# The loads of batch 1 go through the Pool queue, in one order with the weights

## The chip, the cores and the metric

The kernel runs on one core of a Trainium2 chip. The metric is the device time of one execution in microseconds (us). A profile is one execution taken by the hardware profiler; its times count from the start of its span. Engines are named as the profile names them: PE is the matrix engine (PEld its weight loads), DVE the vector engine, ACT the scalar engine, POOL the GpSimd engine, SP the engine that here only issues DMAs. SPq and POOLq are the sequencers of SP and POOL, which wait and issue. DMA queue q1 is fed by SP, queue q0 by POOL, and the same 16 DMA engines serve both.

## The reference: sliding-window attention, then a gated feed-forward

```python
scores = scale * q @ k^T            # B=8, H=8, S=576, D=64
mask   = (0 <= i - j < 64)          # a causal window of 64
attn   = softmax(where(mask, scores, -1e9))
x      = (attn @ v) as [B*S, H*D]   # 4608 tokens x 512
h      = x @ w_in                   # 512 x 2048
out    = (h * clip(h + 3, 0, 6) / 6) @ w_out   # 2048 x 512
```

All inputs and the output are float32. The kernel computes in bf16 with float32 accumulation.

## The kernel before

**Tiles of tokens.** The 4608 tokens are cut into nine tiles of 512 (T = 0 to 8). Each tile has two stages on PE. `s1(T)` multiplies the transposed tokens xT by w_in in 16 column blocks (fc = 0 to 15, four matmuls each, line 530) and gates each block on ACT (line 537) and DVE (line 538) into gT. `s2(T)` multiplies gT by w_out (line 567) into four groups of 128 tokens (ts = 0 to 3). Both are Python generators: each step emits a few instructions, and the code that calls `run(m, n)` places the attention of a coming batch between the steps. The schedule is manual, so each engine does its instructions in the order in which the program lists them.

**Attention of a batch.** A batch has 576 positions, 512 main rows and 64 rest rows. The pieces are: casts of Q, K and V to bf16 on POOL (lines 286, 293, 247); transposes of Q and K on PE, `TT(bt, g)` for a pair of heads g and `RR(bt)` for the rest rows (lines 316, 298), copied out of PSUM by DVE and ACT; scores and exponentials, `S1_(g, half, bank)` (lines 353, 361), masked on DVE (line 371); weighted sums and division by their sum, `N_(bt, g)` (lines 383 to 405); and the transpose into xT, `X_(bt, g)` (line 416). Batches 0 and 1 are transposed on PE. From batch 2 on, Q and K are transposed by DMA, issued by SP: lines 276 to 282 for batch 2, pair by pair, and lines 269 to 274 for batch 3 and later, one transfer for Q and one for K.

**Tile 0.** Tile 0 needs only the main rows of batch 0, so the rest rows of batch 0 are deferred and done inside tile 0 by `RR(bt0)`, `rest_s`, `rest_n`, `rest_x`. During `s1(0)` PE does the first two `TT` of batch 1, and during `s2(0)` the rest of batch 1's attention. `s2(0)` runs in the order BY_PART: four steps with the first quarter of w_out (one for each ts), then four with the second quarter, and so on: 16 steps of four matmuls.

**Loads in tile 0.** The weights come through POOL's queue as four parts of w_in (512 columns each, lines 225 to 229) and four of w_out (512 rows each, lines 231 to 235); they are cast from float32 to bf16 on the way. Each part has 512 rows. Everything else comes through SP's queue, all float32: Q and K of batch 1 in halves of four heads (line 107, 512 rows of 1 KB each), the rest rows of batch 1 (line 113, `rst`, 512 rows of 256 B for Q and as many for K), the rest rows of batch 0 (line 151, three transfers of that kind), then V of batch 1 (lines 94 and 82, 512 rows of 256 B for each of nine transfers), then batches 2, 3, ... (line 94, 1024 rows of 256 B each).

**What sets the order.** The first halves of Q and K of batch 1 wait on SP until the second part of w_in has landed (lines 704, 705). POOL casts that half of Q, issues the first part of w_out, casts the half of K and issues the other three parts of w_out (lines 720 to 723). SP holds `rst` of batch 1, the second halves of Q and K and the rest rows of batch 0 until the first part of w_out has landed (lines 724, 725), and V until the third has (lines 726, 727). POOL casts `rst` (line 728), the second halves (729) and batch 0's rest rows (730). After V, SP issues the loads of batch 2, its transposes, the loads of batch 3, and so on. Staging tiles have one buffer each.

In `s2(0)` before, `RR(bt)` stands after four steps, the last two `TT` after eight.

Of the kernel before, what the change touches and what calls it, by code (L numbers as in the profile page):

```python
# [24 lines left out]
def kernel(  # L25
# [42 lines left out]
    def after(ins, dep, why):  # L68

        tc.add_manual_dep(  # L70
            ins.ins, dep.ins.name,
            mybir.DependencyInfo(mybir.DependencyClass.Sync, mybir.DependencyReason.DATA),
            reason=why,
        )
# [22 lines left out]
            ))  # L97
        return out

    def load_qk_for_pe(b, heads):  # L100
        qst = stage.tile([P, H, R * D], F32, name="qst", tag="qst")
        kst = stage.tile([P, H, R * D], F32, name="kst", tag="kst")
        rst = stage.tile([P, H, D], F32, name="rst", tag="rst")
        ins = []
        for h0 in range(0, H, heads):
            for dst, src in ((qst, q), (kst, k)):
                ins.append(nc.sync.dma_start(
                    out=dst[:, h0 : h0 + heads, :],
                    in_=src[b, h0 : h0 + heads, 0:SM, :].rearrange("h (p j) d -> p h (j d)", j=R),
                ))  # L110
            if h0 == 0:
                for i, src in enumerate((q, k)):
                    ins.append(nc.sync.dma_start(
                        out=rst[i * SR : (i + 1) * SR, :, :],
                        in_=src[b, :, SM:S, :].rearrange("h s d -> s h d"),
                    ))
        return (qst, kst, rst), ins

    def load_v_by_head(b):
        vst = stage.tile([P, KB, H, D], F32, name="vst", tag="vst")  # L120
        ins = load_blocks(vst, v, b, (KB - 1,), SR) + load_v(b, vst, 0, H)
        return vst, ins
# [23 lines left out]
    def load_rest_of_first():  # L146
        rst = stage.tile([P, H, D], F32, name="rst0", tag="rst0")
        rvst = stage.tile([P, H, D], F32, name="rvst", tag="rvst")
        ins = []
        for dst, p0, src in ((rst, 0, q), (rst, SR, k), (rvst, SR, v)):  # L150
            ins.append(nc.sync.dma_start(
                out=dst[p0 : p0 + SR, :, :], in_=src[0, :, SM:S, :].rearrange("h s d -> s h d"),
            ))
        return rst, rvst, ins

    stage0, ins0 = load_first()
    vst0 = stage.tile([P, KB, H, D], F32, name="vst", tag="vst")
# [67 lines left out]
    def load_w_in(f0, f1, g0, g1):  # L225
        return nc.gpsimd.dma_start(
            out=win16[:, g0:g1, f0:f1],
            in_=moe_w_in[g0 * P : g1 * P, f0:f1].rearrange("(g p) f -> p g f", p=P),
        )

    def load_w_out(c0, c1):
        return nc.gpsimd.dma_start(
            out=wout16[:, c0:c1, :],
            in_=moe_w_out[c0 * P : c1 * P, :].rearrange("(c p) j -> p c j", p=P),
        )
# [4 lines left out]
    class Batch:  # L240
        def __init__(self, b):
            self.b = b
            self.QT, self.KT = QT_ring[b % NQT], KT_ring[b % NQT]
            self.V = V_ring[b % NV]
# [181 lines left out]
    def rest_s(bt, u):  # L426
        st = ps_st.tile([P, 2, 512], F32, name=f"st{u}")
        for g in range(NG):
            for h in range(2):
                nc.tensor.matmul(  # L430
                    st[:, h, g * SR : (g + 1) * SR],
                    lhsT=bt.KT[h * D : (h + 1) * D, g, S - P : S],
                    rhs=bt.QT[h * D : (h + 1) * D, g, SM:S], start=True, stop=True,
                )
        nc.scalar.activation(out=pTr[:], in_=st[:, :, 0 : NG * SR], func=EXP, scale=scale)
        pv_ = pTr[:].rearrange("p h (g s) -> p (h g) s", s=SR)
        nc.vector.tensor_tensor(
            out=pv_, in0=pv_,
            in1=mask1[:, WINDOW : 2 * WINDOW].unsqueeze(1).to_broadcast([P, H, SR]), op=MULT,
        )  # L440

    def rest_n(bt, u):
        st = ps_st.tile([P, 2, 512], F32, name=f"st{u}")
        for h in range(2):
            o = st[:, h, :]
            for g in range(NG):
                nc.tensor.matmul(
                    o[0:SR, g * VW : (g + 1) * VW], lhsT=pTr[:, h, g * SR : (g + 1) * SR],
                    rhs=bt.V[:, KB - 1, 2 * g + h, :], start=True, stop=True,
                )  # L450
        for h in range(2):
            ov = st[0:SR, h, 0 : NG * VW].rearrange("p (g w) -> p g w", w=VW)
            rec = small.tile([P, KB], F32, name="rec")
            nc.vector.reciprocal(out=rec[0:SR, 0:NG].unsqueeze(2), in_=ov[:, :, D:VW])
            nc.vector.tensor_tensor(
                out=opr[0:SR, :, h, :], in0=ov[:, :, 0:D],
                in1=rec[0:SR, 0:NG].unsqueeze(2).to_broadcast([SR, NG, D]), op=MULT,
            )

    def rest_x(bt):  # L460
        tr = ps_st.tile([P, 2, 1024], BF16, name="st0")[:, 0, :]
        for g in range(NG):
            nc.tensor.transpose(
                out=tr[:, g * SR : (g + 1) * SR],
                in_=opr[0:SR, g, :, :].rearrange("p h d -> p (h d)"), identity=ident[0:SR, 0:SR],
            )
        acopy(
            out=xT[:, :, bt.b * S + SM : (bt.b + 1) * S],
            in_=tr[:, 0 : NG * SR].rearrange("d (g s) -> d g s", s=SR),
        )  # L470
# [89 lines left out]
    def s2(T, order):  # L560

        gT, accs = gTs[T], {}
        for ts, f0, f1 in order:
            if f0 == 0:
                accs[ts] = h_bank()[:] if T == 0 and ts > 1 else next(oa)
            for fc in range(f0, f1):
                nc.tensor.matmul(  # L567
                    accs[ts], lhsT=gT[:, fc, ts * P : (ts + 1) * P], rhs=wout16[:, fc, :],
                    start=(fc == 0), stop=(fc == NFC - 1),
                )  # L570
            if f1 == NFC:
                osb = osbp.tile([P, DM], F32, name="osb")
                acopy(out=osb[:], in_=accs[ts])  # L573
                u0 = T * TB + ts * P
                if T:
                    nc.sync.dma_start(out=out[u0 : u0 + P, :], in_=osb[:])
                else:
                    held.append((u0, osb))
            yield
# [4 lines left out]
    def run(gen, n=10 ** 6):  # L584
        for _ in range(n):
            if next(gen, "end") == "end":
                break
# [29 lines left out]
    def X_(bt, g, st=None):  # L617
        xt_pe(bt, g, h_tr() if st is None else ps_st.tile([P, 2, 1024], BF16, name=f"st{st}")[:, 0, :])()

    def TT(bt, g, banks=None):  # L620
        T_(bt, g, banks)
        do(bt, "q", g)
        do(bt, "k", g)
# [23 lines left out]
    bt.cast_v(vst0, 4, 6, pcopy)  # L647
    w_in.append(load_w_in(512, 1024, 0, NG))
    bt.cast_v(vst0, 6, 8, pcopy)
    w_in += [load_w_in(512 * i, 512 * (i + 1), 0, NG) for i in (2, 3)]  # L650
    pcopy(out=bt.V[0:SR, KB - 1, :, 0:D], in_=bt.V[SR:P, KB - 2, :, 0:D])

    def S0_(g, u):
# [46 lines left out]
    run(m, 1)  # L700


    st1, ins = load_qk_for_pe(1, 4)
    for x in ins[:2]:
        after(x, w_in[1], "the weights go first")
    bt0 = bt
    rst0, rvst0, insr = load_rest_of_first()
    vst1, insv = load_v_by_head(1)
    insv = insr[2:] + insv

    fill_v(1)
    nc.vector.tensor_copy(
# [5 lines left out]
        )  # L718
    bt, st = Batch(1), st1
    bt.cast_qk(st, 0, 0, 4, pcopy)  # L720
    w_out = [load_w_out(0, 4)]
    bt.cast_qk(st, 1, 0, 4, pcopy)
    w_out += [load_w_out(4 * i, 4 * i + 4) for i in (1, 2, 3)]
    for x in ins[2:] + insr[:2]:
        after(x, w_out[0], "the weights go first")
    for x in insv:
        after(x, w_out[2], "the weights go first")
    bt.cast_rest(st, pcopy)
    cast_pairs(bt, st, 4, 4)
    bt0.cast_rest((None, None, rst0), pcopy)  # L730
    run(m, 12)
    TT(bt, 0, oa_tr)
    run(m, 2)
    TT(bt, 1, oa_tr)
# [8 lines left out]
    def st_tr(u):  # L743
        t = ps_st.tile([P, 2, 1024], BF16, name=f"st{u}")
        return iter((t[:, 0, :], t[:, 1, :]))
# [5 lines left out]
    def S1_(g, u, bank):  # L751
        scores(bt, g, u, bank=bank)()
        if u:
            masked(bt, g)

    m = s2(0, BY_PART)
    S1_(0, 0, 0)
    S1_(1, 0, 1)
    run(m, 4)
    RR(bt, st_tr(0))  # L760
    run(m, 1)
    S1_(0, 1, 1)
    run(m, 1)
    S1_(1, 1, 0)
    run(m, 2)
    TT(bt, 2, st_tr(1))
    TT(bt, 3, st_tr(0))
    run(m, 1)
    S1_(2, 0, 1)
    run(m, 1)  # L770
    S1_(2, 1, 0)
    run(m, 1)
    S1_(3, 0, 1)
    run(m, 1)
    S1_(3, 1, 0)
    run(m, 1)
    RR(bt0, st_tr(1))
    run(m, 1)
    rest_s(bt0, 1)
    N_(bt, 0, st_pair(0))  # L780
    run(m, 1)
    rest_n(bt0, 1)
    N_(bt, 1, oa)
    run(m, 1)
    N_(bt, 2, st_pair(0))
    X_(bt, 0, 1)
    rest_x(bt0)
    X_(bt, 1)
    N_(bt, 3, oa)
    X_(bt, 2)  # L790

# [89 lines left out]
```

## Time and profile before

| what | value |
|---|---|
| time, median of 11 runs | 326.92 us (323.56 to 329.26) |
| time of the profiled execution | 326.03 us, its span 324.3 us |
| PE busy | 304.3 us, 94% of the span |
| POOL busy | 88.7 us, 27% |
| bytes moved by DMA | 52.80 MB, of which queue q1 46.94 MB and q0 5.24 MB |
| PE clock granted, mean | 0.979 |

The page gives the busy time of each engine, and then the span in 40 equal slices with the PE clock and the DMA load of each. A view of waits says who waited for whom; a chain of waits follows the end of the program back to what released each step; a timeline lists instructions as start, duration, engine, line and operands; a table by stretches gives each engine's busy time, the granted clock (1.00 is full speed), the share of the 16 DMA engines and the GB/s. The DMA view gives for each queue the packets, the bytes and the share of the 16 engines' time; the share can exceed 100%, since packets overlap.

### The profile page before, as it was taken

How to read it: one execution, taken by the hardware profiler on the slowest of the kernel's cores; microseconds unless marked ns; L12 is line 12 of the kernel's file. 1: busy time of each engine (PE TensorE's matmuls, PEld its weight loads, DVE VectorE, ACT ScalarE, POOL GpSimd, SP SyncE). 2: the span in 40 equal slices, each digit the busy share in tenths (PEclk: the TensorE clock that was granted, in tenths of full speed). 3: DMA queues.
4: the chain of work that ended last, by engine and by line, in shares of the span. 5: the costliest groups of instructions: out<-in, count | busy, mean ns of one | idle time of the engine just before them, and what ended most of it. 6: DMA issues, size and time to landing. Idle time of an engine off the chain costs nothing.

```text
span 324.3 us, 5582 instructions
## 1 busy us (share of the span) xinstructions
PE 304.3 (94%) x2126; PEld 149.8 (46%) x2162; DVE 175.3 (54%) x334; ACT 177.5 (55%) x264; POOL 88.7 (27%) x128
## 2 busy tenths in 40 slices
PE   8898739979999999999999999999999999999995
PEld 3454214544455445544544454445445544444442
DVE  4668304647664575468726871786177717505800
ACT  2857404537773685379417932793279327416711
POOL 6806028363047043405600353045200000000000
PEclk9999958979999999999999999999999999999999
DMA  7997999999999999899769898999850370020011
GB/s 251 200 202 182 179 250 205 199 236 186 185 194 207 242 213 217 214 183 204 143 167 244 189 204 194 237 189 204 181 134 2 75 138 1 0 99 32 0 67 65
DMA packets 151515, 52.80 MB, mean 163 GB/s; under 512 B 138944, under 2 KB 147136, under 8 KB 151488
## 3 DMA queue, kind: packets, MB, share of 16 engines
q1 hardware_dynamic: 146672, 46.94, 71.9%
q0 software_dynamic: 4544, 5.24, 9.4%
q8 instruction: 17, 0.28, 0.5%
q10 hardware_dynamic: 272, 0.26, 0.2%
q14 instruction: 10, 0.08, 0.1%
HBM read 36.70 MB, written 9.44 MB: 142 GB/s over the span
## 4 chain that ended last, share of the span: by engine, by line
PE 79%; DMA 11%; DVE 4%; ACT 2%; SPq 1%; issue 1%; POOL 1%; POOLq 0%
PE acc L567 18%; PE o L567 18%; PE h L530 15%; PE st L530 6%; PE o L530 6%; PE acc L530 6%; PE st L353 4%; DMA qst<-in_q_dram 4%; DMA rst<-in_k_dram 3%; DMA win<-in_moe_w_in_dram 2%; PE h L383 2%; DVE gT L538 2%; DMA wout<-in_moe_w_out_dram 2%; PE h L388 1%; PE h L567 1%
## 5 line engine op out<-in xcount | busy, mean ns | idle before, releaser
L530 PEld LDWEIGHTS <-win 128*128 128x128 bf16 x576 | 55.7, 98 | 67.0 <-issue 3.2
L567 PEld LDWEIGHTS <-gT 128*128 128x128 bf16 x576 | 53.0, 99 | 58.2 <-issue 2.1
L567 PE MATMUL o<-wout,gT 128*128 128x512 bf16 x261 | 65.0, 383 | 0.8 <-issue 0.3
L567 PE MATMUL acc<-wout,gT 128*128 128x512 bf16 x261 | 63.3, 383 | 0.6
L530 PE MATMUL h<-xT,win 128*128 128x512 bf16 x259 | 62.9, 379 | 0.3
L361 ACT ACTIVATE pT<-st 128x768 bf16<-128x768 f32 x64 | 48.7, 808 | 16.0 <-PE st L353 15.9
L538 DVE SCALAR_TENSOR_TENSOR gT<-t,st 128x512 bf16<-128x512 bf16 (+1 forms) x26 | 20.7, 809 | 59.5 <-ACT t L537 59.5
L537 ACT ACTIVATE t<-h,half 128x512 bf16<-128x512 f32 x66 | 44.7, 691 | 8.4 <-PE h L530 7.9
L538 DVE SCALAR_TENSOR_TENSOR gT<-t,h 128x512 bf16<-128x512 bf16 x66 | 44.6, 685 | 7.9 <-ACT t L537 7.7
L371 DVE TENSOR_TENSOR pT<-pT,mask 128x1536 bf16<-128x1536 bf16 x28 | 29.3, 1046 | 22.9 <-ACT pT L361 22.9
L257 POOL CAST qn<-qst 128x512 bf16<-128x512 f32 x24 | 15.5, 684 | 79.0 <-DMA qst<-in_q_dram 79.0
L573 ACT COPY osb<-acc 128x512 f32<-128x512 f32 x17 | 10.0, 586 | 40.7 <-PE acc L567 40.7
L530 PE MATMUL st<-xT,win 128*128 128x512 bf16 x124 | 30.8, 388 | 0.7 <-DVE gT L538 0.3
L573 ACT COPY osb<-o 128x512 f32<-128x512 f32 x17 | 10.0, 588 | 30.2 <-PE o L567 30.2
L405 DVE TENSOR_TENSOR opg<-h,rec 128x320 bf16<-128x320 f32 x48 | 23.6, 492 | 1.7
L530 PE MATMUL o<-xT,win 128*128 128x512 bf16 x91 | 23.6, 379 | 0.4 <-DVE gT L538 0.3
L530 PE MATMUL acc<-xT,win 128*128 128x512 bf16 x90 | 23.5, 379 | 0.1
L537 ACT ACTIVATE t<-st,half 128x512 bf16<-128x512 f32 (+1 forms) x26 | 20.1, 784 | 6.4 <-PE st L530 6.3
L247 POOL CAST V<-vst 128x512 bf16<-128x512 f32 (+1 forms) x14 | 18.2, 1301 | 14.8 <-DMA vst<-in_v_dram 10.5
L257 POOL CAST kn<-kst 128x512 bf16<-128x512 f32 x24 | 16.5, 726 | 17.3 <-DMA kst<-in_k_dram 17.3
L383 PEld LDWEIGHTS <-pT 128*128 128x128 bf16 x256 | 17.5, 98 | 7.6 <-PE h L416 0.5
L353 PE MATMUL st<-QT,KT 64*128 64x192 bf16 (+2 forms) x312 | 17.8, 233 | 1.0 <-ACT KT L321 0.5
(100 smaller groups left out, 278.7 us busy)
## 6 DMA issues: line engine op xcount, KB each, us to landing
out_dram<-osb SPq DMA_DIRECT2D x32, 256.0 KB, 2.3
qst<-in_q_dram SPq DMA_DIRECT2D x28, 256.0 KB, 4.7
kst<-in_k_dram SPq DMA_DIRECT2D x27, 256.0 KB, 5.3
vst<-in_v_dram SPq DMA_DIRECT2D x24, 256.0 KB, 5.3
vst<-in_v_dram SPq DMA_DIRECT2D x23, 128.0 KB, 3.8
win<-in_moe_w_in_dram POOLq DMA_DIRECT2D x4, 512.0 KB, 7.3
wout<-in_moe_w_out_dram POOLq DMA_DIRECT2D x4, 512.0 KB, 9.2
qst<-in_q_dram SPq DMA_DIRECT2D x2, 512.0 KB, 8.9
```

What stands on the lines that cost most here:

```text
L247: copy(out=self.V[:, 0 : KB - 1, h0:h1, 0:D], in_=vst[:, 0 : KB - 1, h0:h1, :])
L257: pcopy(out=n[:, g, 0 : KB - 1, :, :].rearrange("p k h d -> p k (h d)"), in_=s[:, 0 : KB - 1, 2 * g : 2 * g + 2, :].rearrange("p k h d -> ...
L353: nc.tensor.matmul(st[:, h, o0 : o0 + n], lhsT=bt.KT[h * D : (h + 1) * D, g, k0 : k0 + P], rhs=bt.QT[h * D : (h + 1) * D, g, q0 : q0 + n], ...
L361: nc.scalar.activation(out=pT[:, :, 2 * u : 2 * u + 2, 0:QW], in_=st[:, :, 0:w].rearrange("p h (k w) -> p h k w", k=2), func=EXP, scale=scale,
L371: nc.vector.tensor_tensor(out=pT[:, :, :, 0:QW], in0=pT[:, :, :, 0:QW], in1=mask[:].rearrange("p (h k) w -> p h k w", h=2), op=MULT,)
L383: nc.tensor.matmul(ob, lhsT=pT[:, h, qb, 0:P], rhs=V[:, qb, 2 * g + h, :], start=True, stop=(qb == 0),)
L405: nc.vector.tensor_tensor(out=opgs[bt.b, g][:, 0:nb, h, :], in0=ov[:, :, 0:D], in1=rec[:, 0:nb].unsqueeze(2).to_broadcast([P, nb, D]), op= ...
L530: nc.tensor.matmul(hT, lhsT=win16[:, g, fc * P : (fc + 1) * P], rhs=xT[:, g, t0 : t0 + TB], start=(g == 0), stop=(g == NG - 1),)
L537: nc.scalar.activation(out=t1[:], in_=hT, func=RELU, bias=half[:], scale=1.0 / 6.0)
L538: nc.vector.scalar_tensor_tensor(out=out, in0=t1[:], scalar=1.0, in1=hT, op0=MIN, op1=MULT,)
L567: nc.tensor.matmul(accs[ts], lhsT=gT[:, fc, ts * P : (ts + 1) * P], rhs=wout16[:, fc, :], start=(fc == 0), stop=(fc == NFC - 1),)
L573: acopy(out=osb[:], in_=accs[ts])
```

## The change

The loads of batch 1 except V, and the rest rows of batch 0, are issued by POOL in place of SP, between the weight parts. The order on POOL's queue, after the first two parts of w_in, is now: w_in part 3; first half of Q, then of K; w_in part 4; w_out part 1; `rst` of batch 1 (two transfers); second half of Q, then of K; (casts of the first halves); w_out parts 2 and 3; batch 0's rest rows (three transfers); w_out part 4; (casts of `rst`, of the second halves, of batch 0's rest rows). The waits of lines 704 and 705 and of lines 724 and 725 are gone. V stays on SP and still waits for the third part of w_out.

On PE, the first two `TT` of batch 1 stand one column block earlier in `s1(0)`. In `s2(0)`, `RR(bt)` stands after two steps in place of four, the two `TT` after four and five in place of both after eight, and the pieces after that are spread one between two steps: `RR(bt0)`, `rest_s`, `rest_n`, `N_(bt, 0)`, `N_(bt, 1)` and `rest_x` each have a step between them, and `X_(bt, 0)` stands ahead of `N_(bt, 2)`. `rest_s` uses the PSUM tile st0 in place of st1, and `rest_x` st1 in place of st0.

```diff
-    def load_qk_for_pe(b, heads):
...
+    class LoadsForPE:
...
+        def main(self, i, h0, h1):
+            nc.gpsimd.dma_start(
+                out=self.tiles[i][:, h0:h1, :],
+                in_=(q, k)[i][self.b, h0:h1, 0:SM, :].rearrange("h (p j) d -> p h (j d)", j=R),
+            )
+
+        def rest(self):
+            for i, src in enumerate((q, k)):
+                nc.gpsimd.dma_start(
+                    out=self.rst[i * SR : (i + 1) * SR, :, :],
+                    in_=src[self.b, :, SM:S, :].rearrange("h s d -> s h d"),
+                )
...
-    w_in += [load_w_in(512 * i, 512 * (i + 1), 0, NG) for i in (2, 3)]
+    w_in.append(load_w_in(1024, 1536, 0, NG))
+    ld = LoadsForPE(1)
+    ld.main(0, 0, 4)
+    ld.main(1, 0, 4)
+    w_in.append(load_w_in(1536, 2048, 0, NG))
+    w_out = [load_w_out(0, 4)]
     pcopy(out=bt.V[0:SR, KB - 1, :, 0:D], in_=bt.V[SR:P, KB - 2, :, 0:D])
...
-    st1, ins = load_qk_for_pe(1, 4)
-    for x in ins[:2]:
-        after(x, w_in[1], "the weights go first")
-    bt0 = bt
-    rst0, rvst0, insr = load_rest_of_first()
-    vst1, insv = load_v_by_head(1)
-    insv = insr[2:] + insv
+    ld.rest()
+    ld.main(0, 4, 8)
+    ld.main(1, 4, 8)
+    bt0, st1 = bt, ld.tiles
...
     bt.cast_qk(st, 0, 0, 4, pcopy)
-    w_out = [load_w_out(0, 4)]
     bt.cast_qk(st, 1, 0, 4, pcopy)
-    w_out += [load_w_out(4 * i, 4 * i + 4) for i in (1, 2, 3)]
-    for x in ins[2:] + insr[:2]:
-        after(x, w_out[0], "the weights go first")
+    w_out += [load_w_out(4 * i, 4 * i + 4) for i in (1, 2)]
+    rst0, rvst0 = load_rest_of_first()
+    w_out.append(load_w_out(12, 16))
+    vst1, insv = load_v_by_head(1)
     for x in insv:
         after(x, w_out[2], "the weights go first")
...
-    run(m, 12)
+    run(m, 11)
     TT(bt, 0, oa_tr)
...
     S1_(1, 0, 1)
-    run(m, 4)
+    go(2)
     RR(bt, st_tr(0))
...
-    run(m, 2)
     TT(bt, 2, st_tr(1))
+    go()
     TT(bt, 3, st_tr(0))
...
     RR(bt0, st_tr(1))
-    run(m, 1)
-    rest_s(bt0, 1)
+    go()
+    rest_s(bt0, 0)
+    go()
+    rest_n(bt0, 1)
+    go()
     N_(bt, 0, st_pair(0))
...
```

(`go()` is `run(m, 1)`.)

More of the change, by code (lines that the diff above doesn't have):

```diff
@@ L98, in load_blocks, with __init__ @@
         return out
-    def load_qk_for_pe(b, heads):
[L101 to L117, printed above, removed]
+    class LoadsForPE:
+        def __init__(self, b):
+            self.b = b
+            self.qst = stage.tile([P, H, R * D], F32, name="qst", tag="qst")
+            self.kst = stage.tile([P, H, R * D], F32, name="kst", tag="kst")
+            self.rst = stage.tile([P, H, D], F32, name="rst", tag="rst")
+            self.tiles = (self.qst, self.kst, self.rst)
+        def main(self, i, h0, h1):
[9 more added lines that the diff above has]
+                )
     def load_v_by_head(b):
@@ L148, in load_rest_of_first @@
         rvst = stage.tile([P, H, D], F32, name="rvst", tag="rvst")
-        ins = []
         for dst, p0, src in ((rst, 0, q), (rst, SR, k), (rvst, SR, v)):
-            ins.append(nc.sync.dma_start(
+            nc.gpsimd.dma_start(
                 out=dst[p0 : p0 + SR, :, :], in_=src[0, :, SM:S, :].rearrange("h s d -> s h d"),
-            ))
-        return rst, rvst, ins
+            )
+        return rst, rvst
     stage0, ins0 = load_first()
@@ L458, in rest_n, with rest_x @@
             )
-    def rest_x(bt):
-        tr = ps_st.tile([P, 2, 1024], BF16, name="st0")[:, 0, :]
+    def rest_x(bt, u):
+        tr = ps_st.tile([P, 2, 1024], BF16, name=f"st{u}")[:, 0, :]
         for g in range(NG):
@@ L756, with go @@
     m = s2(0, BY_PART)
+    def go(n=1):
+        run(m, n)
     S1_(0, 0, 0)
     S1_(1, 0, 1)
-    run(m, 4)
+    go(2)
     RR(bt, st_tr(0))
-    run(m, 1)
+    go()
     S1_(0, 1, 1)
-    run(m, 1)
+    go()
     S1_(1, 1, 0)
-    run(m, 2)
+    go()
     TT(bt, 2, st_tr(1))
+    go()
     TT(bt, 3, st_tr(0))
-    run(m, 1)
+    go()
     S1_(2, 0, 1)
-    run(m, 1)
+    go()
     S1_(2, 1, 0)
-    run(m, 1)
+    go()
     S1_(3, 0, 1)
-    run(m, 1)
+    go()
     S1_(3, 1, 0)
-    run(m, 1)
+    go()
     RR(bt0, st_tr(1))
-    run(m, 1)
-    rest_s(bt0, 1)
+    go()
+    rest_s(bt0, 0)
+    go()
+    rest_n(bt0, 1)
+    go()
     N_(bt, 0, st_pair(0))
-    run(m, 1)
-    rest_n(bt0, 1)
+    go()
     N_(bt, 1, oa)
-    run(m, 1)
+    rest_x(bt0, 1)
+    go()
+    X_(bt, 0)
     N_(bt, 2, st_pair(0))
-    X_(bt, 0, 1)
-    rest_x(bt0)
-    X_(bt, 1)
+    X_(bt, 1, 1)
     N_(bt, 3, oa)
```

## The prediction

> **What bounds the kernel now.** I read the page first, then PE's waits, then the chain of waits through the largest of them.
>
> ```profile
> span 324.3 us, 5582 instructions
> PE 304.3 (94%) x2126; PEld 149.8 (46%) x2162; DVE 175.3 (54%) x334; ACT 177.5 (55%) x264; POOL 88.7 (27%) x128
> ...
> PE st L298 <- POOL rn L293: 7.2, 1, 7.2
> PE st L463 <- DVE opg L405: 2.1, 1, 2.1
> ...
> PE acc L316 <- POOL kn L286: 0.9, 1, 0.9
> ```
>
> PE sets the time, and its idle time is nearly all in tile 0. The largest wait is 7.2 us once: RR(bt), the transpose of batch 1's rest rows, waits for their cast. The chain says why the cast is late:
>
> ```profile
> 13.59 6.65 DMA win<-in_moe_w_in_dram
> 20.30 6.70 DMA qst<-in_q_dram
> ...
> 28.13 5.27 DMA wout<-in_moe_w_out_dram
> 33.42 0.72 SPq L113
> ...
> 34.19 10.45 DMA rst<-in_k_dram
> ...
> 44.76 0.62 POOL rn L293
> ```
>
> Loads wait for landings of loads. Between 27.00 (Q lands) and 28.13 (w_out is issued) nothing is queued at all. Then the rest rows, 128 KB, need 10.45 us, because they share the DMA engines with three parts of w_out. The packets of each queue, in stretches 36 to 42, 17.5 to 22.5, 43 to 45.5, 48 to 54 and 70 to 74 us (packets, MB, share of 16 engines):
>
> ```profile
> q0 software_dynamic: 1027, 1.02, 100.8%
> q1 hardware_dynamic: 660, 0.16, 20.9%
> ...
> q0 software_dynamic: 1015, 1.01, 123.5%
> ...
> q1 hardware_dynamic: 877, 0.85, 105.9%
> ...
> q1 hardware_dynamic: 4696, 1.17, 110.7%
> ...
> q0 software_dynamic: 228, 0.75, 58.9%
> ```
>
> The first pair is the rest rows' stretch: 660 small packets of q1 beside 1027 of q0, although q1 alone passes 4696 of them in 6 us. The hole costs more than itself, by the granted clock (stretch, its length, PE, PEld, DVE, ACT, POOL, clock, DMA, GB/s):
>
> ```profile
> 45.00:50.00 5.00, 4.57 (x20) 1.65 (x22) 1.23 (x2) 1.18 (x2) 2.67 (x4) 0.50 1.26 205
> ...
> 50.00:51.00 1.00, 1.00 (x8) 0.49 (x9) 0.22 (x1) 0.53 (x1) 0.94 (x2) 0.50 1.01 188
> 51.00:52.00 1.00, 1.00 (x6) 0.40 (x5) 0.69 (x1) 0.28 (x1) 0.93 (x2) 0.97 1.13 226
> ...
> 68.00:69.00 1.00, 1.00 (x22) 1.00 (x20) 0.63 (x3) 0.70 (x2) 1.00 (x3) 0.56 1.09 211
> ...
> 71.00:72.00 1.00, 1.00 (x4) 0.35 (x3) 0.00 (x0) 0.00 (x0) 1.00 (x3) 0.73 1.17 273
> ```
>
> By the shares in the rows of 51, 68 and 71 us, PE runs at half clock from the hole until 51.05, and after the 2.1-us wait from 68.1 to 71.5.
>
> **What the change can give PE.** It removes the reason for these waits: 0.9 + 7.2 + 2.1 = 10.2 us of idle time. At half clock half of the time is lost: (51.05 - 45.4) / 2 = 2.8 and (71.5 - 68.1) / 2 = 1.7. Together 14.7 us, all before batch 2's attention starts. PE's instructions are the same, only moved.
>
> **When the data now land.** All is one queue, in program order. Prices per 512 rows, from the rows above: a weight part 5 us x 512 / 1015 = 2.52; rows of 1 KB on q1 2.5 x 512 / 877 = 1.46; rows of 256 B on q1 6 x 512 / 4696 = 0.65. The trace shows neither kind of these rows on q0. The bounds are q1's price and the weights' price, 2.52 for both. I choose between them by engine time per packet on q0: a weight row (2 KB read) 1.235 x 5 x 16 / 1015 = 97 ns, a 4-KB output row 0.589 x 4 x 16 / 228 = 165 ns. The straight line gives 63 ns for 1 KB and 38 ns for 256 B, so 2.52 x 63 / 97 = 1.64 and 2.52 x 38 / 97 = 0.99 us. From w_in part 2's landing at 13.59 + 6.65 = 20.24: w_in part 3 22.8; first half of Q 24.4, K 26.0; w_in part 4 28.6; w_out part 1 31.1; rest rows 33.1; second half of Q 34.7, K 36.3; w_out part 2 38.9, part 3 41.4. After that 3 x 0.99 + 2.52 on q0 beside V's nine transfers on q1 (9 x 0.65 = 5.9): 52.8 for the last of V.
>
> **When PE needs them.**
>
> ```profile
> 30.21 1.89 PE L530 MATMUL st<-xT,win 128*128 128x512 bf16 x8
> ...
> 34.20 0.50 PE L353 MATMUL st<-QT,KT 64*128 64x192 bf16 x8
> ...
> 55.74 0.27 PE st L353 x6
> ...
> 59.47 0.22 PE st L298 x4
> ...
> 85.30 1.73 PE o L567 x8
> ...
> 27.15 1.04 POOL L286 CAST qn<-qst 128x1024 bf16<-128x1024 f32 x1 [10.11 <-DMA qst<-in_q_dram]
> ```
>
> Block 12, the first on w_in part 4, started at 30.21, less the 0.9: 29.3 against 28.6. Scores start at 34.20 - 0.9 = 33.3. A step of s2 takes 1.73 / 2 = 0.87, so RR(bt) comes at 33.3 + 0.44 + 1.73 = 35.5, against 34.4: the program has eight completion semaphores for POOL's transfers and uses them in turn, so the last issue ahead of the cast, w_out part 4, the ninth after `rst`'s first, can start only when `rst` has landed at 33.1, and takes 0.7; the cast takes 0.62. TT 2 comes at 35.5 + 0.22 + 2 x (0.87 + 0.27) = 38.0 against 36.3 + 1.04 = 37.4. The second quarter is needed at 38.45 and lands at 38.9: 0.4 wait. The fourth is needed at about 48 and lands between 46.9 and 48. I take 0.8 us of new waits, so PE is 13.9 us earlier at batch 2.
>
> **POOL's queue.** Nine more issues stand on it, and the first-half casts, `rst`'s cast and V's casts are behind them.
>
> ```profile
> 14.90 1.48 POOL L226 DMA_DIRECT2D win<-in_moe_w_in_dram  x2
> ...
> 29.85 2.22 POOL L232 DMA_DIRECT2D wout<-in_moe_w_out_dram  x3
> ```
>
> At 1.48 / 2 = 0.74 each they take 6.7 us. The 10.11 us for which POOL waited for Q before 27.15 (row above) cover them, and its wait from 32.07, the end of the last w_out issue, to 44.76 covers those that come after; without that cover the 6.7 us would delay the casts. I take nothing. SP is freed of nine issues; what was queued behind them there, V and then batch 2, is bound by the landing of w_out part 3 and by the DMA engines.
>
> **What is late next.** The DMA engines stay full until batch 3 is loaded, so PE's 13.9 us are not the gain. V of batch 1 landed last at about 55.5 before, and now at 52.8; everything behind it on SP comes 2.7 us earlier and no more:
>
> ```profile
> 51.74 0.50 SPq L82 DMA_DIRECT2D vst<-in_v_dram  x1
> vst<-in_v_dram SPq DMA_DIRECT2D x7, 128.0 KB, 3.8
> ...
> 72.59 2.08 SPq L279 DMA_TRANSPOSE KT<-kn  x1
> 104.46 3.45 SPq L271 DMA_TRANSPOSE KT<-kn  x1
> KT<-kn SPq DMA_TRANSPOSE x1, 5.4
> ...
> SPq L576 <- ACT osb L573: 81.7, 19, 16.9
> ...
> 86.96 0.51 PE L353 MATMUL st<-QT,KT 64*128 64x192 bf16 x10
> 117.23 0.51 PE L353 MATMUL st<-QT,KT 64*128 64x192 bf16 x10
> ```
>
> (55.5 is the last issue, 51.74, plus 3.8; a transpose of K lands 5.4 after its issue, in both stretches.) Batch 2's first pair landed at 78.0 and was used at 86.96; now it lands at 75.3 and PE is there at 73.1: a wait of 2.2 us, and, as after the 2.1-us wait before, some 1.7 us of clock. Batch 3's K landed at 109.9 and was used at 117.23, 7.3 us later; now it lands at 107.2, and PE arrives at 75.3 + 1.7 + (117.23 - 86.96) = 107.3. Both say the same: **the gain is batch 3's slack plus what the DMA stream wins, 7.3 + 2.7 = 10.0 us.** Later SP waits 81.7 us for output tiles, so its loads have slack from batch 4 on and nothing more binds. Against its own time of 326.03 that is 316.0; the median of the runs lies 0.9 above that execution, so the forecast is 316.9.
>
> **The rivals.**
>
> *PE alone decides.* With q1's prices on q0, V ends 4 x (1.64 - 1.46) + 5 x (0.99 - 0.65) = 2.4 us earlier still, and batch 2 and 3 delay PE less: 7.3 + 5.1 = 12.4 us, and with all waits gone 14: 312.9 to 314.5. For it: q1's rows are measured. Against it: q0's rows cost more engine time by the line.
>
> *Small rows crawl on q0.* At 2.52 for every transfer the stream loses 4 x 0.88 + 5 x 1.53 = 11.2 us, a gain of -1.2; halfway, 10.0 - 5.6 = 4.4: 322.5. For it: nothing small was seen on q0. Against it: 97 against 165 ns shows that size counts. A lost margin at w_in part 4 or TT 2 belongs here, 1 to 3 us.
>
> *POOL's issues stretch, and the kernel is slower.* From w_in part 3 to `rst`'s cast stand 15 issues, 0.6 us of copy and two casts. From 14.90 to 34.9 they have (20.0 - 2.7) / 15 = 1.15 us each; from there on every excess delays RR(bt). If each issue waited for one masked product of DVE (29.3 us over 28, 1.05 each), it would take 1.79, RR(bt) would come 15 x 0.64 = 9.6 us late, the hole would be 2.4 us longer than now, and the DMA queue would run dry: 329.
>
> ```profile
> L371 DVE TENSOR_TENSOR pT<-pT,mask 128x1536 bf16<-128x1536 bf16 x28 | 29.3, 1046 | 22.9 <-ACT pT L361 22.9
> 15.00:20.00 5.00, 4.25 (x64) 2.83 (x62) 4.20 (x16) 2.44 (x5) 1.99 (x3) 1.00 1.21 192
> ```
>
> Against it: the issues at 14.90 took 0.74 with DVE busy 4.20 of 5 us. The Trainium skill (SBUF — State Buffer, A bandwidth-pool intuition that's wrong) warns of just this: a DMA issued by GpSimd takes about 3.1 us in place of 0.62 beside a DVE copy, waiting to write its descriptors. By it the loss would be larger still; these issues do not agree.
>
> *It does nothing measurable.* The stream is late by 7.3 in sum, and the hole moves behind w_out: 326 to 327.
>
> **How the numbers follow.** Forecast 0.52 (own range 314 to 319.5), PE alone 0.17, small rows 0.18 (a third of it no gain or a loss), stretched issues 0.05, nothing 0.03, unnamed mishaps 0.05. A measurement here tells about 0.5%, 1.6 us, from no change. Faster is 0.52 + 0.17 + 0.12 + 0.05 = 0.86; within 0.5% is 0.03 of the small rows and most of the rest, 0.05; slower 0.09, the stretched issues and the last part of the small rows. The range 311 to 322.5 holds the first two and half of the third.
>
> **What would show it.** Right: RR(bt)'s wait is gone and the clock stays at 1.00 from 30 to 60 us; s1(1), begun at 69.07 before, begins at 55 to 56; PE waits on batch 2's or batch 3's transposes, which it does nowhere now; POOL's issues stay near 0.74. Wrong: an issue over 1.15; `rst` landing after 34; no PE wait between 70 and 110 (then the gain is near 14); or V landing after 55.

## The result: 314.11 us, and the profile after

The changed kernel takes 314.11 us (median of 12 runs, 313.1 to 315.3) against 326.87 us (47 runs of the kernel before). The ratio is 0.9647, 95% interval 0.9616 to 0.9678: 12.8 us, 3.5%. The forecast was 316.9 us. The profiled execution of the changed kernel took 314.61 us. The kernel before spreads more, from 322.58 to 329.26 us, and its clock with it: among thirteen of its runs the mean granted clock was 0.989 in one of 323.74 us and 0.978 in one of 327.66.

One thing in the text above is wrong and matters below. In `s2(0)` of the changed code there is one more `go()` ahead of `TT(bt, 2)`: the two `TT` stand after five and six steps, not after four and five, and between `N_(bt, 1)` and `rest_x` there is none. The description of the change has this wrong, and the prediction counted by it.

The page and PE's waits of the changed kernel (its lines are numbered one higher there: 353 is 354, 567 is 568):

```profile
span 312.9 us, 5579 instructions
PE 299.8 (96%) x2125; PEld 148.6 (47%) x2162; DVE 175.7 (56%) x334; ACT 177.4 (57%) x264; POOL 92.4 (30%) x137
...
PE st L354 <- DMA KT<-kn: 1.0, 1, 1.0
PE o L568 <- DMA wout<-in_moe_w_out_dram: 1.0, 1, 1.0
PE h L417 <- DVE opg L406: 0.7, 1, 0.7
```

The waits of 7.2 us (RR(bt)), 2.1 us (rest rows) and 0.9 us (the first `TT`) are gone. In their place are 1.0 us for the second part of w_out and 1.0 us for batch 3's K. Two of the stretches that were shown before, with the granted clock third from the end:

```profile
45.00:50.00 5.00, 4.71 (x38) 2.02 (x38) 2.64 (x5) 2.26 (x4) 2.65 (x4) 1.00 0.87 155
...
68.00:69.00 1.00, 0.95 (x6) 0.41 (x6) 0.82 (x2) 0.71 (x2) 1.00 (x3) 1.00 1.05 245
```

The clock stays at full speed here; in the twelve executions its mean was 0.992 to 1.000. PE's timeline gives where the time came from, by the places named in the prediction:

```profile
39.03 1.02 PE L568 MATMUL o<-wout,gT 128*128 128x512 bf16 x4 [1.03 <-DMA wout<-in_moe_w_out_dram]
...
57.38 1.89 PE L531 MATMUL st<-xT,win 128*128 128x512 bf16 x7
...
74.08 0.51 PE L354 MATMUL st<-QT,KT 64*128 64x192 bf16 x10
...
105.46 0.51 PE L354 MATMUL st<-QT,KT 64*128 64x192 bf16 x10 [1.04 <-DMA KT<-kn]
```

s1(1) begins 69.07 - 57.38 = 11.7 us earlier, batch 2's scores 86.96 - 74.08 = 12.9, batch 3's scores 117.23 - 105.46 = 11.8, and the span is 11.4 us shorter. So the gain is made before s1(3) begins (126.36 us, 138.13 before): from there to PE's last matmul both kernels take the same time within 0.3 us (182.8 and 182.5).

### The profile page after: what moved, and what is told of

Read it like the earlier page. It is cut to its first block, busy times and chain, and to the rows that moved or that the text cites. A ratio compares the mean times of both kernels' runs of the same rounds, so it can differ in the third digit from the quotient of the medians.

```text
span 312.9 us, 5579 instructions
## 1 busy us (share of the span) xinstructions
PE 299.8 (96%) x2125; PEld 148.6 (47%) x2162; DVE 175.7 (56%) x334; ACT 177.4 (57%) x264; POOL 92.4 (30%) x137
## 3 DMA queue, kind: packets, MB, share of 16 engines
q1 hardware_dynamic: 141920, 44.18, 69.6%
q0 software_dynamic: 5360, 8.00, 12.4%
## 4 chain that ended last, share of the span: by engine, by line
PE 72%; DMA 14%; SPq 4%; POOL 3%; DVE 3%; ACT 2%; issue 1%; POOLq 0%
PE acc L568 16%; PE o L568 16%; PE h L531 15%; PE o L531 5%; PE acc L531 5%; PE st L531 5%; DMA wout<-in_moe_w_out_dram 4%; PE st L354 3%; DMA qst<-in_q_dram 3%; DMA kst<-in_k_dram 3%; DMA vst<-in_v_dram 3%; SPq L94 2%; PE h L384 2%; DMA KT<-kn 1%; ACT pT L362 1%
## 5 line engine op out<-in xcount | busy, mean ns | idle before, releaser
L568 PE MATMUL o<-wout,gT 128*128 128x512 bf16 x261 | 64.1, 379 | 1.8 <-DMA wout<-in_moe_w_out_dram 1.0
L568 PE MATMUL acc<-wout,gT 128*128 128x512 bf16 x261 | 62.4, 379 | 0.6
L574 ACT COPY osb<-acc 128x512 f32<-128x512 f32 x17 | 10.0, 586 | 41.4 <-PE acc L568 41.4
L531 PE MATMUL st<-xT,win 128*128 128x512 bf16 x124 | 29.9, 379 | 0.6 <-DVE gT L539 0.3
L248 POOL CAST V<-vst 128x512 bf16<-128x512 f32 (+1 forms) x14 | 16.5, 1180 | 15.8 <-DMA vst<-in_v_dram 13.2
L258 POOL CAST kn<-kst 128x512 bf16<-128x512 f32 x24 | 14.4, 641 | 17.7 <-DMA kst<-in_k_dram 14.0
## 6 DMA issues: line engine op xcount, KB each, us to landing
qst<-in_q_dram POOLq DMA_DIRECT2D x2, 512.0 KB, 11.5
```

What stands on the lines that cost most here:

```text
L248: copy(out=self.V[:, 0 : KB - 1, h0:h1, 0:D], in_=vst[:, 0 : KB - 1, h0:h1, :])
L258: pcopy(out=n[:, g, 0 : KB - 1, :, :].rearrange("p k h d -> p k (h d)"), in_=s[:, 0 : KB - 1, 2 * g : 2 * g + 2, :].rearrange("p k h d -> ...
L531: nc.tensor.matmul(hT, lhsT=win16[:, g, fc * P : (fc + 1) * P], rhs=xT[:, g, t0 : t0 + TB], start=(g == 0), stop=(g == NG - 1),)
L568: nc.tensor.matmul(accs[ts], lhsT=gT[:, fc, ts * P : (ts + 1) * P], rhs=wout16[:, fc, :], start=(fc == 0), stop=(fc == NFC - 1),)
```

## The experiments

Each ratio below is to the kernel before, measured beside it. "Stream" is the sequence of transfers through the DMA engines up to batch 3.

### The loads alone, and PE's order alone

`e1_loads_only` keeps the new queue and puts PE's instructions back into the order of before; `e2_order_only` is the converse, the queue of before with PE's new order.

```diff
 # e1, on the changed kernel
-    run(m, 11)
+    run(m, 12)
     TT(bt, 0, oa_tr)
...
-    go(2)
+    run(m, 4)
     RR(bt, st_tr(0))
...            # the pieces of s2(0) in their former order
```

> The loads of the changed kernel with PE's order of before (RR(bt) after four steps of s2(0), both TT after eight, the norms and the rest rows bunched at the end). Stream theory (the end is set by when the DMA stream delivers batch 3's K, and PE only has to be there in time): K of batch 3 lands at 105 to 106 us as in the changed kernel; PE loses the 2.1-us wait at the rest rows and about 1.7 us of clock after it, less the 1.0 us that it waited for K: 317 to 318 us. If PE's order carries most of the gain: 321 us or more. If the loads carry all of it: 314 to 315.

> The loads of before with PE's order of the changed kernel. Both theories: RR(bt) comes two steps (1.7 us) earlier and its cast no earlier, so its wait grows from 7.2 to about 9 us, the clock halves for as long as before, and the 2.1-us wait at the rest rows goes: 325 to 328 us, no change that counts. If the order carries a good part of the gain by itself: 322 or less.

| kernel | median us | ratio | interval |
|---|---|---|---|
| loads alone | 317.61 (4 runs) | 0.9728 | 0.9651 to 0.9804 |
| order alone | 325.43 (10 runs) | 0.9987 | 0.9946 to 1.0028 |

The largest wait of PE with the loads alone, and then two with the order alone:

```profile
PE st L464 <- DVE opg L406: 2.1, 1, 2.1
```

```profile
PE st L298 <- POOL rn L293: 7.2, 1, 7.2
PE acc L316 <- POOL kn L286: 1.3, 1, 1.3
```

The order alone does nothing that can be told: the hole is where it was (7.2 us, not the 9 us I expected; the steps before it came later, by 1.3 us at the first `TT`). The loads alone carry most of the gain, and their median falls in the 317 to 318 us that the stream theory gave. What the order adds on top, 0.8% by the medians, isn't settled: the interval of the loads alone overlaps that of the whole change. Its four runs hint at the clock. The profiled one is the fastest, 314.75 us, with the clock at 1.00 throughout in spite of the 2.1-us wait, and it ends with the changed kernel (314.61). The other three took 317.43 to 318.02, with mean granted clocks of 0.988 to 0.995. So the order may be worth only what the half clock after that wait costs. Of the other three only the time and the mean clock are known, so this is argued and not shown.

### The rest rows back on SP

Only two transfers move: the 256 KB of rest rows of batch 1 go to SP's queue again and wait for w_out part 1, as before. All else stays as in the changed kernel.

```diff
         def rest(self):
             for i, src in enumerate((q, k)):
-                nc.gpsimd.dma_start(
+                x = nc.sync.dma_start(
...
+                after(x, w_out[0], "as before")
```

> The changed kernel with the two transfers of rest rows of batch 1 back on SP's queue, released by the landing of w_out part 1 as before; everything else stays on POOL's. If sharing the engines packet by packet with the other queue is what made them late: they land at 40 to 43 us in place of 33.1, RR(bt) waits 5 to 8 us, the clock halves, and most of the gain is gone: 321 to 326 us. If only the waits for landings ahead of them made them late: they land at 34 to 36, 314 to 316.5 us.

Measured: 325.62 us, ratio 0.9986 (0.9954 to 1.0018). The whole gain is gone. PE's largest wait, the time to landing of the second transfer (the two are issued at 31.82 and 32.58 us), the packets from 36 to 43 us, and PE's hole in the table of stretches:

```profile
PE st L300 <- POOL rn L295: 10.5, 1, 10.5
...
rst<-in_k_dram SPq DMA_DIRECT2D x1, 128.0 KB, 13.4
...
q0 software_dynamic: 893, 1.13, 92.0%
q1 hardware_dynamic: 886, 0.22, 28.8%
...
41.00:46.00 5.00, 0.00 (x0) 0.00 (x0) 0.00 (x0) 0.00 (x0) 0.00 (x0) 0.56 1.18 180
```

The second transfer lands at 32.58 + 13.4 = 46.0 us, where through POOL's queue it lands at 33.1. That is later than the 40 to 43 us that I expected, and PE waits 10.5 us and not 5 to 8; the time is in the expected range. Two things make it late. From 30 to 35 us q1 passes no packet at all: the first follow the issue by about 4 us, as they did in the kernel before (issued at 33.42, none before 37). From then on the two queues take turns packet by packet, one for one: 886 against 893 here, and 624 against 624 from 38 to 42 us in the kernel before. Since q1's packets carry 256 B and q0's over 1 KB on average, q1 gets 0.22 MB while q0 moves 1.13.

So the chain of landings alone was not what made the rest rows late: issued at the same moment as in the kernel before, relative to w_out part 1, and with nothing else ahead on SP, they are as late again. Being in the one queue, ahead of what is needed later, removes it. Whether an issue on SP long before w_out part 1 lands would do as well was not tried.

### The hole filled

`e5_hole_kept_busy` is the kernel before, with 32 matmuls in the hole whose result nothing reads:

```diff
     run(m, 4)
+    warm = ps_st.tile([P, 2, 512], F32, name="st0")
+    for _ in range(32):
+        nc.tensor.matmul(
+            warm[:, 0, :], lhsT=xT[:, 0, 0:P], rhs=xT[:, 0, 0:TB], start=True, stop=True,
+        )
     RR(bt, st_tr(0))
```

> The kernel before with 32 matmuls of 512 columns, whose result nothing reads, placed on PE ahead of RR(bt), in the hole of 7.2 us. The prediction put 2.8 us on the half clock after the hole. If so, the clock stays at 1.00 from 40 to 60 us, s1(1) begins about 2.8 us earlier than 69.07, and, since batch 3's K has 7.3 us of slack in the kernel before, all of it reaches the end: 323.5 to 324.5 us. If the clock after the hole costs nothing, or if the matmuls delay what waits: 326 to 328.

Measured: 322.08 us (4 runs), ratio 0.9881 (0.9802 to 0.9960), 4.2 us less than the 326.31 beside it and 1.4 us below the range expected; the span of its profiled execution is 320.6. Its timeline and clock:

```profile
46.08 0.38 PE L298 MATMUL st<-ident,rn 128*128 128x128 bf16 x4
...
45.00:51.00 6.00, 5.78 (x45) 2.88 (x45) 2.80 (x3) 2.00 (x3) 3.58 (x5) 1.00 1.29 221
...
66.82 1.46 PE L530 MATMUL st<-xT,win 128*128 128x512 bf16 x5
```

RR(bt) comes at 46.08, 0.65 us later than before (45.43), and still PE arrives at s1(1) 69.07 - 66.82 = 2.25 us earlier. From RR(bt) to s1(1) it needs 20.74 us in place of 23.64: 2.9 us less, where the prediction put 2.8 us on the clock after the hole. In this execution the second stretch of half clock, after the wait at the rest rows, is absent too, although that wait is still 2.0 us long; that is most of the further 1.4 us of the span. Together the prediction priced the two stretches at 2.8 + 1.7 = 4.5 us, and the median moved by 4.2. The mean clock of all four runs is 0.999 or 1.000. What decides whether a wait of 2 us halves the clock, these runs do not show.

### V held back: does the stream set the end?

```diff
     for x in insv:
-        after(x, w_out[2], "the weights go first")
+        after(x, w_out[3], "the weights go first")
```

> The changed kernel with V of batch 1 held on SP until the fourth part of w_out has landed (47.0 us) in place of the third (42.3 us). Stream theory: V ends 2 to 3 us later than 51.9, everything behind it on SP too, batch 3's K lands at 107.5 to 108.5 and PE waits for it: 316 to 317.5 us. PE theory (the end is set by PE's own path through tile 0): V's first casts delay N_(bt, 0) by at most 1 us, nothing else: 314 to 315.2 us.

Measured: 317.58 us (4 runs, 316.29 to 321.26), ratio 0.9732 (0.9653 to 0.9812); the span of the profiled execution is 315.4, 2.5 us more than the changed kernel's. The two places of its timeline:

```profile
76.49 0.51 PE L354 MATMUL st<-QT,KT 64*128 64x192 bf16 x10 [2.53 <-DMA KT<-kn]
...
108.21 0.51 PE L354 MATMUL st<-QT,KT 64*128 64x192 bf16 x10 [1.37 <-DMA KT<-kn]
```

PE comes through tile 0 as in the changed kernel, and then waits 2.5 us for batch 2's first pair and 1.4 us for batch 3's K. Both scores are later by 2.4 and 2.75 us, and the end by 2.5. The intervals of the two ratios overlap by a little, but all four runs lie above all 24 of the changed kernel (its own twelve and those of two repeats, e6 and e11 below), of which the slowest took 315.87. A delay of the stream passes to the end: the stream theory holds in this direction. Its forecast of 316 to 317.5 us is met by the median within 0.1 us.

### Batch 3's wait taken away, and batch 2's

The other direction: PE does something else while it would wait. `e7_scores_later` moves the first scores of batch 3 by two column blocks; `e10_both_scores_later` also moves batch 2's pieces by one step; `e8` is `e7` with V released earlier. `e6` and `e11` are the changed kernel again, as the measure beside them. Each has six runs.

```diff
 # e7 (and e8, e10)
-            return {13: [f(SS, 0)]}, {
+            return {15: [f(SS, 0)]}, {
...
 # e8
-        after(x, w_out[2], "the weights go first")
+        after(x, w_out[1], "the weights go first")
...
 # e10: every step of batch 2's pieces in s2(1) plus one
-                1: [f(SS, 0)], 2: [f(SS, 1)], 4: [f(N_, 0), f(SS, 2)], ...
+                2: [f(SS, 0)], 3: [f(SS, 1)], 5: [f(N_, 0), f(SS, 2)], ...
```

> The changed kernel once more, as the measure for the runs beside it: 314 us, K of batch 3 landing at 105 to 106 and PE waiting for it about 1 us.

> The changed kernel with the first scores of batch 3 two column blocks (1.7 us) later in s1(2), so that PE has other work when it would wait for K. Stream theory: the wait of 1.0 us is gone and reaches the end, 0.7 to 1.0 us less than the changed kernel beside it, 313.0 to 313.5. If something else ends last at that place (batch 2's transposes, ACT, DVE): no difference.

> As the run before it, and V of batch 1 released by the second part of w_out (39 us) in place of the third (42.3). In the changed kernel the DMA engines are not full between 45 and 50 us. If V earlier fills that: V ends 1 to 2.5 us earlier than 51.9, K of batch 3 lands at 103 to 104.5, and the end is 0.5 to 1.5 us below the run before it or equal, as far as PE waits nowhere else. If V only takes turns with the weights: the third or fourth part of w_out lands 1 to 3 us later, PE waits for it in tile 0, and the end is the same or up to 2 us later.

> The changed kernel with the first scores of batch 3 two column blocks later and all attention pieces of batch 2 one step (0.87 us) later in s2(1). With batch 3's scores alone moved, nothing was won: PE waited 0.8 us for batch 2's first pair instead. If both pairs of transposes bind, one as much as the other: no wait over 0.4 us on transposes is left, and the end is 0.7 to 1.3 us below the changed kernel beside it, 312.8 to 313.6 us. If moving the pieces only moves the loss (the norms and copies of batch 2 bunch at the end of the stage, or ACT and DVE come late): no difference.

> The changed kernel once more, as the measure for the run beside it: 314.1 to 314.4 us, with 0.9 to 1.1 us of waits on transposes of batch 2 or batch 3.

| kernel | median us | ratio | interval |
|---|---|---|---|
| changed kernel (e6) | 314.31 | 0.9652 | 0.9603 to 0.9701 |
| batch 3's scores later (e7) | 315.50 | 0.9678 | 0.9637 to 0.9720 |
| and V earlier (e8) | 314.93 | 0.9666 | 0.9622 to 0.9709 |
| changed kernel (e11, beside e10) | 314.73 | 0.9637 | 0.9592 to 0.9681 |
| both scores later (e10) | 314.74 | 0.9642 | 0.9597 to 0.9688 |

The scores of batch 2 and of batch 3 in e6, those of batch 2 in e7, and then waits of PE in e11 and e10:

```profile
74.89 0.51 PE L354 MATMUL st<-QT,KT 64*128 64x192 bf16 x10 [0.95 <-DMA KT<-kn]
...
105.45 0.51 PE L354 MATMUL st<-QT,KT 64*128 64x192 bf16 x10 [0.22 <-DMA KT<-kn]
```

```profile
75.32 0.51 PE L354 MATMUL st<-QT,KT 64*128 64x192 bf16 x10 [0.78 <-DMA KT<-kn]
```

```profile
PE st L354 <- DMA KT<-kn: 1.5, 1, 1.5
```

```profile
PE o L568 <- DMA wout<-in_moe_w_out_dram: 0.7, 1, 0.7
PE st L354 <- ACT pT L362: 0.6, 2, 0.4
```

Where the wait falls changes from one execution to the next. In the first profile of the changed kernel PE waited 1.04 us at batch 3 and not at batch 2; in its repeats it waited at batch 2, 0.95 us in e6 and 1.5 in e11, and 0.22 and nothing at batch 3. So beside e6 the edit of e7 had 0.2 us to win and left the larger wait in place: it decides nothing, and its median is 1.2 us above e6's, inside the intervals. With both moved no wait for a transpose of K is left among the larger ones (beside the one at the kernel's start these are 0.7 us and less). e10 and e11 come through tile 0 alike (s1(1) begins at 58.00 and 57.98), and e10's span is 312.7 against 313.6; but the medians are equal, 314.74 and 314.73, and an effect of 1 us lies within their intervals (about 0.45%, 1.4 us). So the wins that I expected from these waits are not shown. In these traces batch 2's pair, batch 3's K and PE's own work come due within about 1.5 us of each other.

V released earlier did not help: SP issues it at 39.2 us in place of 42.3, and its nine transfers take until 49.5.

```profile
39.19 0.72 SPq L94 DMA_DIRECT2D vst<-in_v_dram  x1
39.96 9.59 SPq L82 DMA_DIRECT2D vst<-in_v_dram  x8
49.67 4.75 SPq L94 DMA_DIRECT2D qst<-in_q_dram  x5
```

Batch 2's loads follow at 49.67, against 49.95 in the changed kernel. V was released 3.1 us earlier and the stream behind it moved by 0.3 us: batch 3's K is issued at 101.18, against 101.06. That fits V and the weights taking turns.

## Why the prediction was right, step by step

**The hole and its cause: right, with one part missing.** All three waits went, and moving the rest rows alone brings the largest back and the whole time with it. The prediction had the sharing of the engines; that the first packets come only about 4 us after the issue is in its 10.45 us without being named. Nor was nothing queued between 27.00 and 28.13: the first half of K was under way until 20.76 + 7.8 = 28.6. But the engines did run empty, with 3 packets from 28 to 29 us.

**The landings on POOL's queue: right within 1 us.** The issues on POOL, each with the wait before it where there was one:

```profile
15.90 0.76 POOL L109 DMA_DIRECT2D qst<-in_q_dram  x1
16.65 0.77 POOL L109 DMA_DIRECT2D kst<-in_k_dram  x1
17.39 0.78 POOL L227 DMA_DIRECT2D win<-in_moe_w_in_dram  x1
18.13 0.80 POOL L233 DMA_DIRECT2D wout<-in_moe_w_out_dram  x1
...
20.41 0.71 POOL L116 DMA_DIRECT2D rst<-in_k_dram  x1
...
23.68 0.75 POOL L109 DMA_DIRECT2D kst<-in_k_dram  x1 [1.78 <-DMA win<-in_moe_w_in_dram]
...
27.49 1.50 POOL L233 DMA_DIRECT2D wout<-in_moe_w_out_dram  x2
...
31.75 0.69 POOL L152 DMA_DIRECT2D rst<-in_k_dram  x1 [2.05 <-DMA wout<-in_moe_w_out_dram]
...
34.13 0.62 POOL L294 CAST rn<-rst 128x512 bf16<-128x512 f32 x1
```

and the time to landing of some of them, in the DMA view:

```profile
qst<-in_q_dram POOLq DMA_DIRECT2D x1, 512.0 KB, 9.0
kst<-in_k_dram POOLq DMA_DIRECT2D x1, 512.0 KB, 9.7
win<-in_moe_w_in_dram POOLq DMA_DIRECT2D x1, 512.0 KB, 11.3
wout<-in_moe_w_out_dram POOLq DMA_DIRECT2D x1, 512.0 KB, 13.3
rst<-in_k_dram POOLq DMA_DIRECT2D x1, 128.0 KB, 12.7
kst<-in_k_dram POOLq DMA_DIRECT2D x1, 512.0 KB, 13.0
wout<-in_moe_w_out_dram POOLq DMA_DIRECT2D x1, 512.0 KB, 11.5
```

| what | predicted | issue + time to landing |
|---|---|---|
| first half of Q | 24.4 | 15.90 + 9.0 = 24.9 |
| w_in part 4 | 28.6 | 17.39 + 11.3 = 28.7 |
| w_out part 1 | 31.1 | 18.13 + 13.3 = 31.4 |
| rest rows | 33.1 | 20.41 + 12.7 = 33.1 |
| second half of K | 36.3 | 23.68 + 13.0 = 36.7 |
| w_out part 2 | 38.9 | 27.49 + 11.5 = 39.0 |
| cast of the rest rows done | 34.4 | 34.13 + 0.62 = 34.75 |

The largest miss is w_out part 3, which releases V: 41.4 was predicted, and SP issued V at 42.33.

**POOL's issues: right.** They took 0.69 to 0.80 us among these rows, 0.74 was taken, 1.15 would have been the point of danger. The rival of stretched issues falls: DVE was busy 3.70 of the 4 us from 16 to 20, and the issues there took 0.71 to 0.80. They do not agree with the sentence of the Trainium skill (SBUF — State Buffer, A bandwidth-pool intuition that's wrong) that the prediction set beside this rival; that holds for these transfers beside these DVE operations, and no run here shows others. The waits of 1.78 and 2.05 us fit the eight semaphores, all in use: each ends 0.3 us after the landing of the transfer eight issues back, w_in part 3 at 23.4 and w_out part 1 at 31.4. The casts behind them still waited for data, 0.64 and 0.39 us for the first halves.

**The wait for w_out part 2: the count was wrong.** 0.4 us was predicted and 1.03 measured. The prediction left out the step ahead of `TT(bt, 2)`: the fifth step comes at 38.0, right after the scores, and not behind a `TT`. The landing itself was right.

**PE through tile 0: 1 us too high, and the mark for s1(1) miscounted.** s1(1) was to begin at 55 to 56 and began at 57.38. That mark did not follow from the prediction's own sum: the half clock from 69.07 to 71.5, 1.2 of the 14.7 us, lies behind the start of s1(1), so with 0.8 us of new waits the sum gives 69.07 - 12.7 = 56.4. The place to compare is batch 2's scores, where 13.9 us were forecast and 12.9 measured. The new waits took 1.8 us in place of 0.8: 1.03 us for w_out part 2, and 0.7 us, not foreseen, for `opg`, the divided sums of the attention that DVE hands to `X_` (third wait in the first fence).

**The stream: the term that was mis-sized.** V was to land 2.7 us earlier, and batch 3's K with it, at 107.2. The last issues of V, the issue of the two transposes of K, and how long each took to land, in the changed kernel:

```profile
48.73 1.06 SPq L82 DMA_DIRECT2D vst<-in_v_dram  x2
vst<-in_v_dram SPq DMA_DIRECT2D x1, 128.0 KB, 2.7
...
68.50 1.66 SPq L280 DMA_TRANSPOSE KT<-kn  x1
KT<-kn SPq DMA_TRANSPOSE x1, 5.5
...
101.06 2.77 SPq L272 DMA_TRANSPOSE KT<-kn  x1
KT<-kn SPq DMA_TRANSPOSE x1, 4.4
```

V's last transfer, the second of the first row, lands at 48.73 + 0.53 + 2.7 = 52.0, 3.5 us earlier than before; predicted were 52.8 and 2.7. V was released 0.9 us late, so the stretch from its release to its end took 9.7 us where the prices gave 11.4: that is the term that was too large. Batch 3's K lands at 101.06 + 4.4 = 105.5, 4.4 us earlier: 3.4 of that stood at its issue (104.46 before), and 1.0 came from a landing that took 4.4 in place of 5.4. The slack of 7.3 us was right. So 7.3 + 4.4 = 11.7 for 7.3 + 2.7 = 10.0, against 11.8 measured at batch 3's scores. The 1.0 us of the landing was in no term of the prediction. It is there in both repeats too (4.3 and 4.5 us); why these landings are faster is not shown.

That the DMA engines stay full until batch 3 is loaded was wrong in both kernels. While SP issues batch 2's transposes, one after the other, the loads of batch 3 stand behind them and the engines have room; in the changed kernel:

```profile
75.00:80.00 5.00, 4.75 (x51) 2.60 (x51) 3.20 (x6) 3.96 (x7) 0.00 (x0) 1.00 0.59 134
```

The last two numbers are the share of the DMA engines and the GB/s; in the kernel before, 80 to 85 us had 0.61 and 138. So the order of SP's queue, and not only full engines, passes V's 3.5 us on to batch 3's K almost whole.

**The wait at batch 2 and its clock: not as predicted.** 2.2 us of wait and 1.7 us of half clock were put there. K of the first pair landed at 68.50 + 5.5 = 74.0 and PE was there at 74.08, so nothing was waited for in that execution, and 0.95 and 1.5 us in the two repeats. The half clock followed in none of these profiles, nor after the 2.5 us of the kernel with V held back. Since the 1.7 us only filled a wait for batch 3's K, it would not have shown at the end.

**That the stream sets the end: half shown.** Holding it back by 2 to 3 us cost 2.5 us, as forecast. The other half, that PE would end earlier if the stream did not hold it, is not shown: with no wait on the stream left, e10 ended with the changed kernel. The rival in which PE alone decides was priced at 312.9 to 314.5, and the measured 314.11 lies in that band, and only 0.1 us inside the forecast's own range of 314 to 319.5. The two limits meet here, and the time cannot tell them apart. The rival's condition, q1's prices on q0, came true for the rows of 1 KB (1.5 us for 512; q1 1.46, forecast 1.64) and half for those of 256 B (0.85; q1 0.65, forecast 0.99).

**Small rows on q0: the rival falls.** Neither kind of row paid the price of a weight row, 2.52 us for 512: the 1024 rest rows took 33.1 - 31.4 = 1.7 us, 0.85 for 512, and those of 1 KB 1.5 (see below).

**From the profile to the median.** The prediction assumed that the median would lie 0.9 us above the profiled execution, as before. It lies 0.5 below (314.11 against 314.61). So 2.8 us between forecast and result are 1.4 of mechanism (11.4 in place of 10.0, from 326.03 to 314.61) and 1.4 of this assumption. That the two have the same sign is chance, and one execution does not tell its place among the others.

## What to carry to other kernels

Here two queues that shared the DMA engines took turns packet by packet, so a transfer of many small packets, issued while the other queue was full of large ones, came late although it was needed first (128 KB took 10.4 and 13.4 us). Put into the same queue, ahead of what was needed later, it landed in the order of issue, and that order could be summed from prices per row within 1 us. Before a gain on the busiest engine is booked, find the next place where data come just in time: the gain ends where the slack there does, plus what the stream itself wins. When two such limits lie within a microsecond or so of each other, as here, taking one away need not show, and which of them binds can change from run to run: compare with a profile of the unchanged kernel from the same round.

## What the runs showed of the hardware that was not expected

**POOL's queue joins rows.** The prediction took one packet per row, as the weights and SP's queue have. In the changed kernel, from 23 to 25 us (mostly Q and K, rows of 1 KB) and from 30.5 to 33 us (mostly rest rows of 256 B):

```profile
q0 software_dynamic: 222, 0.70, 104.0%
...
q0 software_dynamic: 197, 0.62, 102.3%
```

That is over 3 KB a packet in both. Over the whole execution the kernel with the rest rows back on SP settles it: there the 1024 rest rows add 1056 packets to q1 (142976 against 141920) and take away 96 from q0 (5264 against 5360). So on q0 they make a tenth of the packets. The price per byte was no gain for the rows of 1 KB: Q's half landed at 24.9 and K's at 16.65 + 9.7 = 26.4, 1.5 us for 512 rows of 1 KB, as on q1. The Trainium skill (DMA: Bandwidth & Descriptors, SWDGE vs HWDGE vs iDMA) states that a packet built on GpSimd has preferably up to 4096 B and up to 64 descriptors; these rows agree with the size.

**A wait of 2 us may or may not halve the clock.** In the profile of the kernel before the half clock followed a wait of 2.1 us (68.1 to 71.5). It did not follow 2.0 us with the hole filled, 2.1 us with the loads alone (the fastest of its four runs), or 2.5 us with V held back:

```profile
57.00:62.00 5.00, 4.17 (x47) 2.73 (x49) 1.97 (x7) 2.29 (x4) 2.56 (x5) 1.00 1.36 213
```

```profile
76.50:80.00 3.50, 3.25 (x29) 1.65 (x31) 1.13 (x2) 3.13 (x5) 0.00 (x0) 1.00 0.61 135
```

(the loads alone, behind the wait at the rest rows; V held back, behind the wait for batch 2's pair). The Trainium skill (TensorE: Matmul & The Clock Gate, Part 1) states that the clock is set by how busy PE was in windows of about 3.4 us that run freely. That would fit a wait which counts in one execution and not in another; where a window began can't be seen in these rows. A wait of 2.1 us is shorter than such a window, so no window was idle from end to end, and how much activity in it keeps the clock up no run here shows.
